# Memory attention, dense MoE and soft MoE in one kernel: five of eight chunks of M by VectorE turns, logits for two chunks at a time in the last batch, and another cut of the output stores

## The chip, the cores and the metric

The kernel runs on one core of a Trainium2 chip. The metric is device time in microseconds (us) of one execution. A core has a matrix engine (TensorE, PE in the profile, with its weight loads as PEld), VectorE (DVE), ScalarE (ACT), GpSimd (POOL) and SyncE (SP). DMA transfers are issued from a queue of an engine: here all of them are issued from SP's.

## The reference, cut to what matters

Three stages follow each other. `S` is 576 rows per batch, there are 4 batches.

```python
a = softmax(phi, axis=2)                       # over 32 memory slots
k_m, v_m = einsum(a, k), einsum(a, v)          # 32 x 64 per head
x = softmax(q @ k_m.T / 8) @ v_m               # attention, then heads side by side: (2304, 512)

p = domain_probs / domain_probs.sum(-1)
out = sum(p[:, e:e+1] * (relu(x @ w1[e]) @ w2[e]) for e in range(4))    # w1 512x1024, w2 1024x512

logits = out @ phi2                            # 32 slots
d = softmax(logits, axis=0); slot_input = d.T @ out
slot_out[e] = relu(slot_input[e] @ v1[e]) @ v2[e]                       # 8 experts, 4 slots each
return softmax(logits, axis=1) @ slot_out      # (2304, 512)
```

## The kernel before, in words

`out` of the middle stage is never built. The kernel keeps the hidden values h of the four experts and uses `M = w2 @ phi2` (32 columns for each of the 4096 hidden units, held as eight chunks of 512 units) so that the logits come straight from h. The slot input is gathered from h and multiplied by w2 only at the end.

The work on a batch goes in chunks n = 0 to 7, two for each expert. For each chunk, `g_mult` multiplies w1 by the batch's memory values (L695, with copies L704 and L706), and four `up` steps make h: each runs six matmuls of 288 columns for every half of the batch (L770 to L772), a ScalarE relu into an `hts` tile (L778), a VectorE 32x32 block turn into h (L784), and a GpSimd multiplication by the expert's share (L788). `logits` (L806; L813 in the last batch) multiplies the four `hts` tiles of a chunk by M and adds two chunks of an expert in one PSUM bank, which `expert` reads (L891). `group` then makes the column softmax of a batch and sums h with it (L976). Batches 0 to 2 are one unit each with both halves of the rows; the last batch is two units of 288 rows, and for these `logits` runs after each chunk, with four matmuls of 32x288.

`m_chunk` makes a chunk of M while batch 0 runs: one 1 MB load of w2 by SP, 16 TensorE transposes of 128x128 in four groups (L837) that ScalarE and VectorE copy out (L847, L843), four matmuls against phi2 (L854), a ScalarE copy (L860), four matmuls that fold and turn the result (L866) and a VectorE copy into M (L871). The chunks use the places R[3] and R[4] in turn, so a chunk's load waits until the chunk two before it has been read.

After the last `group` the end stage streams w2, v1 and v2 from memory in 1 MB blocks (`load_block`, `refill`) through buffers that the main loop gives up, makes the 32 slot outputs, and multiplies them by the row softmax: 20 result blocks of up to 128x512 (L1361, one PSUM bank each), copied out by VectorE (L1366) and ScalarE (L1369) in turn, and sent by SP (L368). The slot outputs lie in `so4`, whose left half ScalarE copies (L1347) and whose right half VectorE copies (L1349).

The order of the instructions on every engine is written by a planner (`Plan`): each step has an engine, an assumed cost, what it reads and writes, and a due time `at`; the planner plays the program through with these and puts each engine's steps out in the order in which they start there. On the chip every engine, SP's queue too, works through its list in that order and waits at a step whose input is late. Places in SBUF that a step may choose from (`uses`) are given out by `Uses` from the lifetimes in the order of due times.

## Time and profile before

| | us |
|---|---|
| median of 3 runs | 508.97 (508.2 to 511.94) |
| the profiled execution, device time | 507.71 |
| its span, first to last instruction | 505.9 |
| PE busy in the span | 476.3 |
| output stores in the span | 12, of 4.72 MB together |

The profiled execution is a fourth one. The profile gives the busy time of each engine, a chain of work followed back from the last instruction (each piece is what the next one waited for, or the instruction before it on its engine), the instructions grouped by line and shape, and the busy time, granted TensorE clock and DMA traffic of any stretch. The lines that the chain names tell the stages: L837 to L871 belong to M, L770 to L772 to `up`, L813 to the last batch's logits, L1361 to the result.

### The profile page before, as it was taken

To read this page: it belongs to the slowest core of one execution; us is meant where nothing else is said; L and a number is where in the kernel's file an instruction comes from. 1 tells how busy PE (TensorE), PEld (TensorE's weight loads), DVE (VectorE), ACT (ScalarE), POOL (GpSimd) and SP (SyncE) were. 2 spreads that over 40 slices of the span, in tenths; PEclk is the share of its full clock that TensorE was granted. 3 is DMA by queue.
4 is the path that set the end of the run, shared out by engine and by line. 5 is a ranking of instruction groups with operands and counts; after the bars stand their busy time and mean duration, and the time that the engine had idled before them with its cause. 6 is when DMAs were issued, how large, how long until landed. Compare 5 with 4: busy or idle time off the path is not lost.

```text
span 505.9 us, 13222 instructions
## 1 busy us (share of the span) xinstructions
PE 476.3 (94%) x5592; PEld 338.2 (67%) x5592; DVE 297.1 (59%) x605; ACT 202.7 (40%) x475; POOL 212.1 (42%) x255
## 2 busy tenths in 40 slices
PE   3999999999999999999999999999999989999971
PEld 2677787777876788788668887775687866333230
DVE  6588546656685857767684676586677553100032
ACT  2354445555550555455245555433543330010031
POOL 0244224546651348775324778532773850000000
PEclk9999999999999999999999999999999999899996
DMA  7999866415420946362082645525345988999938
GB/s 223 235 352 315 331 173 204 153 34 179 165 85 4 319 118 185 106 188 84 3 265 86 205 168 179 197 85 195 97 130 202 356 302 328 412 426 419 421 127 332
DMA packets 65243, 106.08 MB, mean 210 GB/s; under 512 B 28576, under 2 KB 40864, under 8 KB 59552
## 3 DMA queue, kind: packets, MB, share of 16 engines
q1 hardware_dynamic: 65184, 105.23, 60.9%
q8 instruction: 44, 0.72, 0.6%
q14 instruction: 15, 0.12, 0.1%
HBM read 100.50 MB, written 4.72 MB: 208 GB/s over the span
## 4 chain that ended last, share of the span: by engine, by line
PE 78%; DMA 14%; SPq 3%; DVE 2%; ACT 1%; issue 1%; DVEq 0%; ACTq 0%
PE ps L770 15%; PE ps L771 13%; PE ps L772 13%; PE ps L976 8%; DMA v<-in_moe_w_dram 8%; PE ps L695 6%; PE ps L806 5%; DMA h<-in_moe_w_dram 3%; PE ps L837 3%; SPq L368 3%; DMA raw<-in_moe_w_dram 3%; PE ps L813 2%; PE ps L854 2%; PE ps L603 2%; PE ps L615 2%; PE ps L866 1%
## 5 line engine op out<-in xcount | busy, mean ns | idle before, releaser
L788 POOL TENSOR_TENSOR h<-h,pe 128x576 f32<-128x576 f32 (+1 forms) x160 | 157.7, 996 | 141.5 <-DVE h L784 117.6
L770 PE MATMUL ps<-A,g 128*128 128x288 f32 x512 | 158.0, 309 | 0.2 <-ACT hts L778 0.2
L778 ACT ACTIVATE hts<-ps 128x288 f32<-128x288 f32 x256 | 105.1, 412 | 130.4 <-PE ps L772 129.0
L771 PE MATMUL ps<-A,g 128*128 128x288 f32 x512 | 151.1, 295 | 0.0
L772 PE MATMUL ps<-A,g 128*128 128x288 f32 x512 | 150.9, 295 | 0.0
L784 DVE STREAM_TRANSPOSE h<-hts 128x576 f32<-128x576 f32 (+1 forms) x160 | 102.4, 647 | 53.5 <-ACT hts L778 53.0
L770 PEld LDWEIGHTS ps<-A,g 128*128 128x128 f32 x512 | 96.1, 188 | 23.9 <-issue 18.6
L771 PEld LDWEIGHTS ps<-A,g 128*128 128x128 f32 x512 | 96.2, 188 | 0.3 <-POOL A L657 0.2
L772 PEld LDWEIGHTS ps<-A,g 128*128 128x128 f32 x512 | 96.1, 188 | 0.0
L706 DVE TENSOR_TENSOR g<-ps,g 128x512 fp32r<-128x512 f32 x64 | 41.0, 678 | 20.0 <-ACT g L704 19.9
L704 ACT CAST g<-ps 128x512 fp32r<-128x512 f32 x64 | 34.9, 590 | 34.5 <-PE ps L695 33.8
L976 PE MATMUL ps<-h,dts 32*32 32x512 f32 x1152 | 40.0, 597 | 1.6 <-DVE dts L958 1.6
L695 PE MATMUL ps<-raw,vbs 64*32 64x512 f32 x512 | 35.9, 600 | 1.6 <-DVE g L706 0.9
L976 PEld LDWEIGHTS ps<-h,dts 32*32 32x32 f32 x1152 | 22.8, 103 | 15.2 <-issue 4.6
L806 PE MATMUL ps<-hts,M 128*32 128x288 f32 x384 | 28.2, 411 | 0.0
L632 POOL TENSOR_TENSOR atts<-atts,small 128x256 f32<-128x256 f32 (+1 forms) x20 | 11.5, 575 | 25.7 <-DVE small L630 25.6
L837 PE MATMUL ps<-ident,h 128*128 128x128 f32 x128 | 18.1, 278 | 0.2 <-DVE g L706 0.2
L806 PEld LDWEIGHTS ps<-hts,M 128*32 128x32 f32 x384 | 10.4, 109 | 10.6 <-issue 5.1
L643 POOL TENSOR_TENSOR atts<-atts,small 128x256 f32<-128x256 f32 (+1 forms) x20 | 11.5, 575 | 13.4 <-DVE small L641 6.3
L837 PEld LDWEIGHTS ps<-ident,h 128*128 128x128 f32 x128 | 14.5, 143 | 2.4 <-issue 1.4
L894 POOL TENSOR_TENSOR lts<-lts,pe 128x288 f32<-128x288 f32 x15 | 10.4, 691 | 12.6 <-DMA v<-in_moe_w_dram 9.4
L657 POOL TENSOR_TENSOR A<-atts,A 128x256 fp32r<-128x256 f32 (+1 forms) x20 | 13.6, 680 | 4.4 <-ACT A L655 4.4
(185 smaller groups left out, 508.6 us busy)
## 6 DMA issues: line engine op xcount, KB each, us to landing
raw<-in_moe_w_dram SPq DMA_DIRECT2D x32, 1024.0 KB, 5.2
v<-in_moe_w_dram SPq DMA_DIRECT2D x20, 1024.0 KB, 12.5
h<-in_moe_w_dram SPq DMA_DIRECT2D x18, 1024.0 KB, 8.4
h<-in_k_dram SPq DMA_DIRECT2D x8, 512.0 KB, 5.2
h<-in_v_dram SPq DMA_DIRECT2D x8, 512.0 KB, 7.1
atts<-in_moe_w_dram SPq DMA_DIRECT2D x4, 1024.0 KB, 9.0
atts<-in_q_dram SPq DMA_DIRECT2D x12, 256.0 KB, 5.6
atts<-in_phi_dram SPq DMA_DIRECT2D x8, 256.0 KB, 4.7
```

The costliest lines, as they stand in the source:

```text
L695: nc.tensor.matmul(bank[bs[c]][32 * i:32 * i + 32, :], vb[b % 2][64 * c:64 * c + 64, 32 * i:32 * i + 32], t()[64 * c:64 * c + 64, i, :], s ...
L704: add(ACT, act(512), lambda c=c, src=src: nc.scalar.copy(out=placed(g()[:, 2 * c]), in_=src), r=[pk(bs[c])], w=[wk(o + 1024 * c, 512)], at ...
L706: add(DVE, dve(512), lambda c=c, src=src: nc.vector.tensor_tensor(out=placed(g()[:, 2 * c + 1]), in0=src, in1=placed(g()[:, 2 * c].bitcast ...
L770: nc.tensor.matmul(t, gh, ah, start=(c == 0), stop=False)
L771: nc.tensor.matmul(t, gh, al, start=False, stop=False)
L772: nc.tensor.matmul(t, gl, ah, start=False, stop=(c == 1))
L778: add(ACT, act(w), lambda: nc.scalar.activation(out=t[:, o0 - base:o1 - base], in_=bank[bm][:, 0:w], func=ACTF.Relu,), r=[pk(bm)], w=[wk(h ...
L784: add(DVE, dve(width), lambda: nc.vector.transpose(out=h_of(u, e)[:, kx], in_=t), r=[wk(ho, width)], w=[hk], at=at + 0.4)
L788: add(POOL, pool(width), lambda: nc.gpsimd.tensor_tensor(out=h_of(u, e)[:, kx], in0=h_of(u, e)[:, kx], in1=share, op=ALU.mult), r=["pe"], ...
L806: nc.tensor.matmul(lb[r0:r0 + 32, 0:HB], M[:, 4 * n + a, :], at_place(hos[a] + o0, o1 - o0), start=(first and h == 0), stop=(not first and ...
L837: nc.tensor.transpose(bank[bk][:, 128 * c:128 * c + 128], wn()[:, a, 128 * c:128 * c + 128], ident)
L976: nc.tensor.matmul(bank[S0 + p][32 * c:32 * c + 32, :], dtv[rows, tb, :], h_pair(u, ep)[rows, :, :, tb, :], start=(tb < 2), stop=(tb >= nt ...
```

## The change

It has three parts. Chunks 3 to 7 of M (the fourth to the eighth) no longer use `m_chunk` but a new `m_turned`: w2's chunk is loaded in four pieces of 32 partitions and 256 KB each, in runs of 1 KB; VectorE turns it in four block transposes of 128x512; TensorE makes 32 matmuls of 64 rows, 32 output partitions and 128 columns from a second copy of phi2 (`load_phi2`, four small loads), into one bank, the first 64 rows into its lower and the other 64 into its upper half; VectorE turns the result into M. For the last batch, `logits` runs after every second chunk, with the eight matmuls of both; `hts` places are then handed out in steps of 288. In the end stage the first row block of batches 0 and 1 is made in two column halves, the blocks are sent in other pieces and another order (`send`), and the four remainders of 64 rows are sent earlier in that order, from GpSimd's queue.

```diff
--- before.py
+++ after.py
...
@@ -364,8 +361,8 @@
     small_at.o = 0
-    def dma(to, of, size, r=(), w=(), at=0.0, cost=0.6):
-        add(SP, cost, lambda: nc.sync.dma_start(
+    def dma(to, of, size, r=(), w=(), at=0.0, cost=0.6, eng=SP):
+        add(eng, cost, lambda: (nc.sync if eng == SP else nc.gpsimd).dma_start(
             out=to() if callable(to) else to, in_=of() if callable(of) else of,
         ), r=r, w=w, at=at, size=size)
@@ -772,7 +769,8 @@
                 nc.tensor.matmul(t, gl, ah, start=False, stop=(c == 1))
         add(PE, 0.81, f, r=[wk(go, 2048)] + a_part(b, 0, o0, w) + a_part(b, 1, o0, w), w=[pk(bm)], at=at, lag=None)
         if ki == 0:
-            ht_of[u, n, fb] = uses(*[HT + 576 * n for n in range(NHT)])
+            step = 576 if len(ranges) == 2 else 288
+            ht_of[u, n, fb] = uses(*range(HT, HT + 576 * NHT, step), width=step)
         ho = ht_of[u, n, fb]
         t = at_place(ho, width)
         add(ACT, act(w), lambda: nc.scalar.activation(
@@ -794,7 +792,8 @@
         base = ranges[0][0]
         first = n % 2 == 0
         lb = bank[LB]
-        hos = [ht_of[u, n, a] for a in range(4)]
+        n0 = n if len(ranges) == 2 else n - 1
+        hos = [ht_of[u, m, a] for m in range(n0, n + 1) for a in range(4)]
         def f():
             if len(ranges) == 2:
@@ -809,15 +808,68 @@
                                 start=(first and h == 0), stop=(not first and h == 1),
                             )
             else:
-                for a in range(4):
+                for m, ho in enumerate(hos):
                     nc.tensor.matmul(
-                        lb[32 * a:32 * a + 32, 0:HB], M[:, 4 * n + a, :], at_place(hos[a], HB),
-                        start=first, stop=not first,
+                        lb[32 * (m % 4):32 * (m % 4) + 32, 0:HB], M[:, 4 * n0 + m, :], at_place(ho, HB),
+                        start=m < 4, stop=m >= 4,
                     )
         width = ranges[-1][1] - base
-        add(PE, 1.05 * len(ranges) / 2 + 0.05, f,
-            r=[("M", n)] + [wk(o, width) for o in hos], w=[pk(LB)], at=at, lag=0)
+        add(PE, 1.1, f,
+            r=[("M", m) for m in range(n0, n + 1)] + [wk(o, width) for o in hos], w=[pk(LB)], at=at, lag=0)
+    def phi_of():
+        return at_place(R[4] + 4096, 256).rearrange("p (c s) -> p c s", c=8)
+    def load_phi2(at):
+        for p in range(4):
+            dh = p % 2
+            dma(
+                lambda p=p: phi_of()[32 * p:32 * p + 32],
+                phi2[256 * dh:256 * dh + 256].rearrange("(c i) s -> i c s", i=32),
+                32768, w=[("phi2", p)] + ([wk(R[4] + 4096, 256)] if p == 0 else []), at=at,
+            )
+    def m_turned(n, ats):
+        e, f = divmod(n, F // FH)
+        o = R[3 + n % 2]
+        def wn(q, w):
+            return at_place(o + 512 * q, 512 * w)
+        def wt():
+            return at_place(o + 2048, 2048).rearrange("p (y a c h x) -> p h c a x y", y=2, a=4, c=8, h=2)
+        for p in range(4):
+            fh, dh = divmod(p, 2)
+            src = w2[e, FH * f:FH * f + FH, 256 * dh:256 * dh + 256]
+            src = src.rearrange("(h x k) d -> h x k d", h=2, k=8)[fh]
+            dma(
+                lambda p=p: wn(0, 4)[32 * p:32 * p + 32].rearrange("p (k d) -> p k d", k=8), src,
+                262144, w=[("wn", o, p)] + ([wk(o, 2048)] if p == 0 else []), at=ats[0] + 0.001 * p,
+            )
+        for a in range(4):
+            add(DVE, dve(512), lambda a=a: nc.vector.transpose(
+                out=at_place(o + 2048 + 512 * a, 512), in_=wn(a, 1)),
+                r=[wk(o + 512 * a, 512)] + [("wn", o, p) for p in range(4)],
+                w=[wk(o + 2048 + 512 * a, 512)], at=ats[1 + a])
+        bk = g_bank()
+        def part():
+            for c in range(8):
+                for q in range(4):
+                    rows = slice(64 * (q // 2), 64 * (q // 2) + 64)
+                    nc.tensor.matmul(
+                        bank[bk][32 * q:32 * q + 32, 0:128], phi_of()[rows, c, :], wt()[rows, q % 2, c],
+                        start=(c == 0), stop=(c == 7),
+                    )
+        add(PE, 2.3, part, r=[wk(o + 2048, 2048), wk(R[4] + 4096, 256)] + [("phi2", p) for p in range(4)],
+            w=[pk(bk)], at=ats[5])
+        add(DVE, 0.3, lambda: nc.vector.transpose(
+            out=M[:, 4 * n:4 * n + 4].rearrange("p a s -> p (a s)"), in_=bank[bk][:, 0:128],
+        ), r=[pk(bk)], w=[("M", n)], at=ats[5] + 0.1)
@@ -1148,9 +1201,10 @@
         add(PE, 0.3, lambda x=x, bk=bk: spread(x, bk), r=["dpn", "cst"], w=[pk(bk)], at=2.5 + x)
         add(DVE, 1.1 if x == 3 else 0.5, lambda x=x, bk=bk: tables(x, bk), r=[pk(bk)], w=["pe"], at=2.6 + x)
+    load_phi2(6)
     m_at = [2.5, 6.2, 10.5, 14.5, 18.5, 22.5, 26.5, 30.5]
     for n, m0 in enumerate(m_at):
-        m_chunk(n, [m_at[n - 2] + 1.6 if n > 1 else n - 181.5, m0, m0 + 0.5, m0 + 1, m0 + 1.5, m0 + 2.4, m0 + 3.2])
+        (m_chunk if n < 3 else m_turned)(n, [m_at[n - 2] + 1.6 if n > 1 else n - 181.5, m0, m0 + 0.5, m0 + 1, m0 + 1.5, m0 + 2.4, m0 + 3.2])
@@ -1172,7 +1226,8 @@
                     up(u, n, fb, ki)
             if u < NU - 1 and s + 1 < NG:
                 g_mult(s + 1, place(u, n, 1) + 0.1)
-            logits(u, n, place(u, n + 1) + (0.6 if n < NCH - 1 else 1.6))
+            if n % 2 or len(ranges) == 2:
+                logits(u, n, place(u, n + 1) + (0.6 if n < NCH - 1 else 1.6))
             if n % 2:
                 expert(u, n // 2, place(u, n + 1) + 1.7)
         z = starts[u + 1]
@@ -1354,46 +1409,57 @@
     spare = spare[:5]
     nres = [0]
-    def result(b, o, rows_out, ot, ok, at):
+    def result(b, o, rows_out, ot, cs, ok, at):
         rows = slice(32 * b, 32 * b + 32)
         bk = uses(*MM, LB, S0, S0 + 1, S0 + 2, S0 + 3)
-        m = rows_out.stop - rows_out.start
+        m, w = rows_out.stop - rows_out.start, cs.stop - cs.start
         add(PE, 0.3, lambda: nc.tensor.matmul(
-            bank[bk][0:m, :], ct[rows, o:o + m], so4[rows, :], start=True, stop=True,
-        ), r=[("ct", b), ("so4", 0), ("so4", 1)], w=[pk(bk)], at=at)
+            bank[bk][0:m, 0:w], ct[rows, o:o + m], so4[rows, cs], start=True, stop=True,
+        ), r=[("ct", b)] + [("so4", n) for n in range(2) if cs.start < 256 * n + 256 and 256 * n < cs.stop],
+            w=[pk(bk)], at=at)
         nres[0] += 1
         if nres[0] % 2:
-            add(DVE, dve(512), lambda: nc.vector.tensor_copy(out=ot(), in_=bank[bk][0:m, :]), r=[pk(bk)],
+            add(DVE, dve(w), lambda: nc.vector.tensor_copy(out=ot(), in_=bank[bk][0:m, 0:w]), r=[pk(bk)],
                 w=[ok], at=at + 0.01)
         else:
-            add(ACT, act(512), lambda: nc.scalar.copy(out=ot(), in_=bank[bk][0:m, :]), r=[pk(bk)], w=[ok],
+            add(ACT, act(w), lambda: nc.scalar.copy(out=ot(), in_=bank[bk][0:m, 0:w]), r=[pk(bk)], w=[ok],
                 at=at + 0.01)
+    def send(b, r0, r1, at):
+        t, o = spare[b]
+        dma(
+            out[b * S:b * S + 512, :].rearrange("(p r) d -> p r d", r=4)[:, r0:r1, :],
+            lambda: t()[:, r0:r1, :], 262144 * (r1 - r0), r=[wk(o + 512 * r0, 512 * (r1 - r0))], at=at,
+        )
     at = zz + 3
-    for r0 in (0, 2):
-        for b0 in (0, 2):
-            for x in range(2):
-                for b in (b0, b0 + 1):
-                    t, o = spare[b]
-                    i = r0 + x
-                    result(b, 128 * i, slice(0, 128), lambda t=t, i=i: t()[:, i, :], wk(o + 512 * i, 512), at)
+    whole_row = (slice(0, 512),)
+    for bs, rs in (((0, 1), (0,)), ((2, 3), (0, 1)), ((0, 1), (1,)), (None, None), ((0, 1), (2, 3)), ((2, 3), (2, 3))):
+        if bs is None:
+            t, o = spare[4]
+            for b in range(B):
+                rows_out = slice(64 * (b % 2), 64 * (b % 2) + 64)
+                k_ = ("tail", b)
+                result(
+                    b, 512, rows_out, lambda t=t, b=b, rows_out=rows_out: t()[rows_out, b // 2, :], whole_row[0], k_, at
+                )
+                dma(
+                    out[b * S + 512:b * S + 576, :], lambda t=t, b=b, rows_out=rows_out: t()[rows_out, b // 2, :],
+                    131072, r=[k_], w=[wk(o + 512 * b, 512)], at=at + 0.05, cost=1.0, eng=POOL,
+                )
+                at += 0.1
+            continue
+        for i in rs:
+            for b in bs:
+                t, o = spare[b]
+                for cs in halves if (b, i) in ((0, 0), (1, 0)) else whole_row:
+                    result(
+                        b, 128 * i, slice(0, 128), lambda t=t, i=i, cs=cs: t()[:, i, cs], cs,
+                        wk(o + 512 * i + cs.start, cs.stop - cs.start), at,
+                    )
                     at += 0.1
-            for b in (b0, b0 + 1):
-                t, o = spare[b]
-                dma(
-                    out[b * S:b * S + 512, :].rearrange("(p r) d -> p r d", r=4)[:, r0:r0 + 2, :],
-                    lambda t=t, r0=r0: t()[:, r0:r0 + 2, :], 524288, r=[wk(o + 512 * r0, 1024)], at=at,
-                )
-    t, o = spare[4]
-    for b in range(B):
-        rows_out = slice(64 * (b % 2), 64 * (b % 2) + 64)
-        k_ = ("tail", b)
-        result(b, 512, rows_out, lambda t=t, b=b, rows_out=rows_out: t()[rows_out, b // 2, :], k_, at)
-        dma(
-            out[b * S + 512:b * S + 576, :], lambda t=t, b=b, rows_out=rows_out: t()[rows_out, b // 2, :], 131072,
-            r=[k_], w=[wk(o + 512 * b, 512)], at=at + 0.05,
-        )
-        at += 0.1
+        for b in bs:
+            send(b, rs[0], rs[-1] + 1, at)
```

The order that comes out of the planner differs at these places. TensorE, batch 0, around a chunk of M. `ps_96` and `ps_97` are the two banks that M and g_mult share, `h_103` is the place of w2's chunk, L837 and L889 the transposes, L854 and L866 the product and the fold, L864 the new product. Before (the last group of transposes of one chunk, its product and its fold, with batch 1's memory sums L514 between them):

```order
L837 MATMUL ps_97<-ident,h_103 128x128 x4
L557 MATMUL ps_98<-ident,atts 128x128
L514 MATMUL ps_99<-h_89,atts 32x64 x16
L519 MATMUL ps_99<-atts 32x64 x4
L854 MATMUL ps_96<-h_103,phi_sb 32x512 x4
L514 MATMUL ps_98<-h_89,atts 32x64 x16
L519 MATMUL ps_98<-atts 32x64 x4
L866 MATMUL ps_97<-si,ct 128x32 x4
```

Now (two chunks' products follow each other, then the memory sums L511 and the next g_mult L692):

```order
L768 MATMUL ps_93<-A,g 128x288
L769 MATMUL ps_93<-A,g 128x288
L864 MATMUL ps_97<-h_103 32x128 x32
L864 MATMUL ps_96<-h_103 32x128 x32
L511 MATMUL ps_98<-h_89,atts 32x64 x16
L516 MATMUL ps_98<-atts 32x64 x4
L692 MATMUL ps_97<-raw,vbs 32x512
```

The product of a chunk is one row of 32 matmuls where a group of transposes, a product and a fold stood, and all eight chunks are through after 25 `up` steps of one half, where they took 38.

VectorE at about the same place of the program (L784 and L782 are the turns of h, L843 copies a group of transposes out, L871 and L924 copy M, L706 and L703 make g, L891 and L944 read the logits). Before:

```order
L784 STREAM_TRANSPOSE h_89<-hts 128x576
L871 COPY M<-ps_97 128x128
L891 STREAM_TRANSPOSE lts<-ps_95 128x288
L843 COPY h_103<-ps_97 128x4x128 x2
L561 COPY kbs<-ps_98 64x128 x2
L871 COPY M<-ps_97 128x128
L784 STREAM_TRANSPOSE h_89<-hts 128x576 x2
L706 TENSOR_TENSOR g<-ps_96,g 128x512
```

Now (L854 are the turns of w2, L870 those of the product into M):

```order
L924 COPY M<-ps_97 128x128
L854 STREAM_TRANSPOSE h_103<-h_103 128x512
L944 STREAM_TRANSPOSE lts<-ps_95 128x288
L854 STREAM_TRANSPOSE h_103<-h_103 128x512 x2
L870 STREAM_TRANSPOSE M<-ps_96 128x128
L854 STREAM_TRANSPOSE h_103<-h_103 128x512 x3
L782 STREAM_TRANSPOSE h_89<-hts 128x576
L854 STREAM_TRANSPOSE h_103<-h_103 128x512 x2
```

Six turns of w2 stand between two turns of h (the first of these is one row ahead of the piece), and a turn of w2 waits for its chunk's load. SP now issues the five chunks as 20 loads, the last two chunks ahead of batch 2's phi, where they stood behind it, and phi2's second copy as four more around batch 1's phi.

SP at the end of the program, the stores. Before:

```order
L368 DMA h_89<-in_moe_w_dram 128x2048 x2
L368 DMA out_dram<-h_89 128x1024 x2
L368 DMA out_dram<-atts 128x1024 x2
L368 DMA out_dram<-h_89 128x1024 x2
L368 DMA out_dram<-atts 128x1024 x2
L368 DMA out_dram<-v 64x512 x4
```

Now, with the four stores of 64x512 in GpSimd's list:

```order
L365 DMA out_dram<-h_89 128x512 x2
L365 DMA out_dram<-atts 128x1024 x2
L365 DMA out_dram<-h_89 128x512 x2
L365 DMA out_dram<-h_89 128x1024 x2
L365 DMA out_dram<-atts 128x1024 x2
```

The first two stores are half as large, and the remainders are no longer the last.

## Rows read from the trace of the kernel before

**Rows 1.** The page: TensorE's busy time, and the chain's shares by engine.

```profile
PE 476.3 (94%) x5592; PEld 338.2 (67%) x5592; DVE 297.1 (59%) x605; ACT 202.7 (40%) x475; POOL 212.1 (42%) x255
...
PE 78%; DMA 14%; SPq 3%; DVE 2%; ACT 1%; issue 1%; DVEq 0%; ACTq 0%
```

**Rows 2.** Stretches (us): length, busy per engine, granted clock, DMA share, GB/s.

```profile
60.00:90.00 30.00, 29.94 (x354) 24.06 (x351) 16.57 (x31) 14.61 (x32) 10.64 (x11) 1.00 0.66 204
432.00:488.00 56.00, 51.70 (x348) 17.51 (x340) 3.60 (x15) 4.46 (x8) 0.00 (x0) 0.97 0.93 384
420.00:425.00 5.00, 4.37 (x80) 2.88 (x62) 2.73 (x7) 0.00 (x0) 0.00 (x0) 1.00 0.55 184
```

**Rows 3.** The chain of waits from 61.5 to 111 us, shares by line.

```profile
by line: PE ps L837 18.9%; PE ps L770 14.1%; PE ps L771 12.3%; PE ps L772 12.3%; PE ps L854 10.3%; PE ps L866 10.0%; PE ps L806 6.4%; PE ps L695 5.2%; PE ps L603 4.1%; PE ps L615 3.1%; ACT ct L860 1.2%; PE ps L514 1.2%; PE ps L519 0.5%; PE 
```

**Rows 4.** The chain: four transposes of M, and the logits at 25 up steps.

```profile
61.90 0.47 PE ps L837 x4
...
81.17 0.97 PE ps L806 x16
```

**Rows 5.** The chain: 16 instructions of 128x32 by 128 columns.

```profile
76.16 0.59 PE ps L615 x16
...
88.80 0.47 PE ps L615 x16
```

**Rows 6.** Groups by line and shape: count, busy us, mean ns, idle before.

```profile
L784 DVE STREAM_TRANSPOSE h<-hts 128x576 f32<-128x576 f32 x96 | 73.6, 768 | 37.4 <-ACT hts L778 37.0
...
L784 DVE STREAM_TRANSPOSE h<-hts 128x288 f32<-128x288 f32 x64 | 28.8, 467 | 16.1 <-ACT hts L778 16.0
...
L843 DVE COPY h<-ps 128x512 f32<-128x512 f32 x16 | 10.9, 679 | 5.5 <-PE ps L837 5.3
```

**Rows 7.** Stretches as in rows 2: the loads of M, the stores.

```profile
46.00:60.00 14.00, 13.78 (x183) 10.02 (x181) 9.32 (x17) 6.65 (x15) 3.59 (x3) 1.00 0.99 348
492.00:502.00 10.00, 2.79 (x18) 0.67 (x14) 4.00 (x7) 3.22 (x7) 0.00 (x0) 0.77 1.02 406
502.00:505.00 3.00, 0.00 (x0) 0.00 (x0) 0.00 (x0) 0.00 (x0) 0.00 (x0) 0.50 0.70 219
```

**Rows 8.** Timeline: a chunk's transposes, and the issue of its load.

```profile
54.33 1.07 PE L837 MATMUL ps<-ident,h 128*128 128x128 f32 x8 [0.22 <-DVE g L706]
46.33 2.15 SPq L368 DMA_DIRECT2D h<-in_moe_w_dram  x2
```

**Rows 9.** Groups by shape: the last batch's logits.

```profile
L813 PE MATMUL ps<-hts,M 128*32 128x288 f32 x128 | 11.6, 418 | 0.0
```

**Rows 10.** The chain: logits of 16 instructions, and the next up's pieces.

```profile
324.06 1.11 PE ps L806 x16
325.17 0.33 PE ps L770
325.89 0.14 PE ps L771
```

**Rows 11.** The chain: logits of 8 instructions, and the next up.

```profile
391.94 0.62 PE ps L813 x8
392.57 0.33 PE ps L770
```

**Rows 12.** Timeline of the end: start, length, engine, line, what.

```profile
487.42 0.37 ACT L1347 COPY kbs<-ps 128x256 f32<-128x256 f32 x1 [0.79 <-PE ps L1343]
...
488.45 6.33 PE L1361 MATMUL ps<-kbs,ct 32*128 32x512 f32 x40 [0.61 <-DVE kbs L1349]
...
489.58 0.69 DVE L1366 COPY h<-ps 128x512 f32<-128x512 f32 x1 [1.27 <-PE ps L1361]
489.67 0.59 ACT L1369 COPY h<-ps 128x512 f32<-128x512 f32 x1 [1.87 <-PE ps L1361]
...
491.16 0.82 SPq L368 DMA_DIRECT2D out_dram<-h  x2
...
499.15 3.86 SPq L368 DMA_DIRECT2D out_dram<-v  x4
```

More of the change, by code (lines that the diff above doesn't have):

```diff
@@ L157, in __init__, with __call__ @@
         self.found, self.kinds = None, []
-    def __call__(self, *places):
+    def __call__(self, *places, width=1):
         uid = len(self.kinds)
-        self.kinds.append(places)
+        self.kinds.append((places, width))
         return Use(self.found[uid] if self.found else places[0], uid)
@@ L170, in settle @@
                     life.setdefault(uid, [n, n, s[0], s[0]])[1::2] = [n, s[0]]
-        taken = {}
-        found = {}
-        order = sorted(life, key=lambda uid: (len(self.kinds[uid]) > 1, life[uid]))
+        taken, found = [], {}
+        order = sorted(life, key=lambda uid: (len(self.kinds[uid][0]) > 1, life[uid]))
         for uid in order:
             a, z = life[uid][:2]
+            places, width = self.kinds[uid]
             best = None
-            for place in self.kinds[uid]:
-                held = taken.setdefault(place, [])
-                if all(z < lo or hi < a for lo, hi, _ in held):
-                    last = max((hi for _, hi, _ in held if hi < a), default=-1)
+            for place in places:
+                held = [h for h in taken if h[2] < place + width and place < h[2] + h[3]]
+                if all(z < h[0] or h[1] < a for h in held):
+                    last = max((h[1] for h in held if h[1] < a), default=-1)
                     if best is None or last < best[0]:
                         best = (last, place)
-            assert best is not None, (
-                self.kinds[uid], life[uid],
-                [(life[o][2:], o) for p in self.kinds[uid] for lo, hi, o in taken[p] if not (z < lo or hi < a)],
-            )
+            assert best is not None, (places, life[uid])
             found[uid] = best[1]
-            taken[best[1]].append((a, z, uid))
+            taken.append((a, z, best[1], width))
         self.found, self.kinds = found, []
@@ L839, in flip @@
                     )
-            add(PE, 0.42, flip, r=[wk(o + 512 * a, 512), "cst"], w=[pk(bk)], at=ats[1 + a])
+            add(PE, 0.42, flip, r=[wk(o + 512 * a, 512), "cst"] + [("wn", o, p) for p in range(4)], w=[pk(bk)],
+                at=ats[1 + a])
             src = bank[bk].rearrange("p (c f) -> p c f", c=4)
```

1 line of the change is left out of this document (removed).

## The prediction

> **What bounds the kernel now.** I read the page first: TensorE is busy for 476 of 505.9 us, and the chain that ends last is 78% TensorE and 14% DMA [rows 1]. A share of the whole span says nothing about one stage, so I took stretches next. From 60 to 90 us, where M is made beside batch 0, TensorE is busy 29.94 of 30 us while VectorE has 16.57 and the DMA engines a share of 0.66: only TensorE's work counts there, as long as data come in time. From 432 to 488 us it is the other way round: DMA share 0.93 at 384 GB/s [rows 2], the stream of w2, v1 and v2, where TensorE's time is worth nothing. Between the two, at 420 to 425 us, the DMA share is 0.55 [rows 2]: no transfers are left over when the last batch's sums end, so the stream starts as soon as these free its buffers, and what the main loop saves ahead of it moves the end one for one. Last I read the chain itself for M's steps, the logits and the stores.
>
> **M's chunks 3 to 7, what goes.** The chain from 61.5 to 111 us holds these five chunks and nothing of the first three. Of its 49.5 us, the transposes L837 take 18.9%, the product L854 10.3%, the fold L866 10.0%, and the wait for ScalarE's copy L860 1.2% [rows 3]: 9.4 + 5.1 + 5.0 + 0.6 = 20.0 us, or 4.0 a chunk. One group of a chunk's transposes stands in [rows 4].
>
> **What comes on TensorE.** A chunk has 32 matmuls, 64 instructions in the profile's two passes. The nearest rows are L615: 8 matmuls of 32 output partitions and 128 columns, 16 instructions, in 0.47 or 0.59 us [rows 5], four at a time in the four column groups. Four times that is 1.9 to 2.4 us; I take 2.1. It could not be had for less than 1.9, since the columns and the groups are the same. The other end is 3.8, twice 1.9, if the products from the lower 64 rows do not run beside those from the upper 64; no row shows two row halves writing one bank. Five chunks: 10.5 us, a gain of **9.5 us**.
>
> **What comes elsewhere.** A turn of 512 columns lies between VectorE's 467 ns for 288 and 768 for 576 [rows 6]: 0.70 us. 20 of them are 14.0 us; the 10 copies L843 that go, at 0.68 [rows 6], are 6.8. 7 us more on VectorE fit into its 13 idle us of the stretch, but its list is strict: a turn that waits for its load holds up the turn of h behind it, then the `hts` places, then `up`. ScalarE only loses copies. SP gets 19 more issues; two loads took it 2.15 us at 46 us [rows 8], so these may hold its queue for up to 20 us, spread over the 50 in which it now waits for other things, with w1's blocks and batch 1's k and v behind them. The M transposes at 54.33 us waited for VectorE's L706, not for their load [rows 8], so the loads are in time now, but from 46 to 60 us the DMA engines are full, share 0.99 at 348 GB/s [rows 7].
>
> **Late data.** The five chunks are wanted earlier (the order ends M after 25 `up` steps, today 81 us [rows 4], not 38), and in pieces of 32 partitions with 1 KB runs. No row has such a load. The nearest are the stores at the end: 128 partitions run at 406 GB/s for a share of 1.02, the 64-partition remainders at 219 for 0.70 [rows 7], 398 against 313 for a full share. So 1 MB costs 2.6 us of DMA at best and, as a bound, twice that. Twice it is 13 us more for five chunks, against 10 idle us of 60 to 90 (0.34 of 30): 3 us that nothing covers, and some waits out of turn. Between 0 and 3 I take **+1.5 us**. On this the Trainium skill, page "SBUF — State Buffer", section "Door 1: The DMA port swizzle", speaks against the change: 32 partitions reach 8 of 16 ports, and it lists 189 GB/s for 1 MB there against 328 for 128 partitions. By it five loads would take 1.7 times as long, 9.5 us more and nearly all of the idle time; I would then put the term at 2 and the sum below at -11.5, where the 128-partition rate alone gives 0 and -13.5.
>
> **The last batch's logits.** 128 instructions are 16 steps of 8 [rows 9], each 0.62 us, and the first piece of the next `up` is 0.33 instead of the usual 0.14 [rows 10, 11]. Merged, 16 instructions take 1.11 [rows 10]: 16 x 0.62 - 8 x 1.11 = 1.0 us, and 0.2 for each switch that goes. Of 8, I count 6, since g_mult breaks the `up` steps at some of these places anyway: 1.2. Together **-2.2 us**, between -1.0 and -2.7. Cover is not needed: it is all TensorE's own time. The steps of the eight tiles hold `hts` longer, but there are now 12 places of 288 columns; if VectorE fell behind, `up` would wait for a place.
>
> **The stores.** Now the first result matmul starts at 488.45, the first copy at 489.58, and the first store goes out at 491.16, after two rounds of copies of 0.69 us [rows 12]. With halves, the left one needs only ScalarE's copy, done at 487.79 (487.42 + 0.37), and the right one starts as today; of the lag of 1.13 us about half goes with the columns. So the right half is copied from 489.0 to 489.6 on, 0.35 us long, and the first store goes at about 489.7, 1.5 us sooner. The DMA engines then drain 4.72 MB at 406 GB/s without a gap until 502, and carry the remainders at 219 to 505 [rows 7]. The two first stores are 0.52 MB, 1.3 us of that; a gap of a few tenths may follow, since the next four blocks need two more rounds. The remainders, now in the middle, may give back up to 1.4 of their 3 us. Between -1.0 and -2.7 I take **-1.8 us**. GpSimd's store is an operation that this trace does not have. SP's remainders go out from 499.15 on [rows 12]; the new ones can go some 6 us sooner, so a GpSimd issue that is 6 us slower than SP's costs nothing, and a faster one gains nothing, as the stream is full.
>
> **Sum:** -9.5 + 1.5 - 2.2 - 1.8 = -12.0 us on a profiled execution of 507.71, so 495.7. The median of the runs is 1.26 us above that execution, so I forecast **497.0 us** against 508.97.
>
> **Rivals.**
> - *A, data in time and everything at its good end:* gains of 10.5, 2.7 and 2.7 us, 493 us. For it: DMA has idle time and VectorE too. Chance 0.08 for below 493.
> - *B, M's gain goes into waits for its data:* VectorE's strict list stands behind each load, so that a late chunk costs `up` as well as its own product. 1.3 us at each of five products beyond the 1.5 makes 6.5: 503.5. For it: the DMA engines are full at 46 to 60 us, and the order wants M a third sooner. Against it: 10 idle us behind. Chance 0.14.
> - *C, the two row halves take turns:* 3.8 instead of 2.1 us for five products is 8.5 us, less the late data that this covers: 504. For it: all other row-split matmuls of this kernel write a bank for each row group. The Trainium skill, page "TensorEngine Tiling (Array Packing)", section "Gotcha 1: PSUM Pressure", has it as a rule that row tiles cannot access one bank at the same time; by it C would hold, or the halves would have to be kept apart in another way. Against it: the halves write different partitions. Chance 0.10.
> - *D, slower than before:* pieces of 32 partitions move at a quarter of the rate of 128, about 100 GB/s. 1 MB then takes 10 us; the five, which share two places, come in one row from 48.5 us on [rows 8], with two blocks of w1 of 2.6 us between them. The last lands at 104 and is turned at 107, where TensorE, at 25 `up` steps, stands at about 83, 2 us later than today [rows 4] for the products that are moved ahead. It waits 24 us in one sum: 497 - 1.5 + 24 is 519.5. It decides from about 8 us a chunk on; the 64-partition stores, at 0.8 of the rate for a full share, are far from that. Chance 0.04.
> - That the change does not do what it says is out: the order has five products, eight merged logits, and the new stores.
>
> The forecast itself, from 493 to 501, has 0.64. The range takes in most of B and the middle of C, **492.5 to 504**: outside lie some of A, the upper ends of B and C, and D, together about 0.2. 1% is 5.1 us, which is about what a measurement tells from no change. Below 503.9 lie the forecast, A, half of B and half of C: faster 0.85; the rest of B and C within 1%: 0.11; slower 0.04.
>
> **What would show it.** In the changed profile: a product of M (L864) of 32 matmuls at 1.9 to 2.4 us (C: near 3.8); no line between 28 and 90 us in which TensorE waits for VectorE or a load for more than 1.5 us in all (B and D: waits of L864 for the turns L854, and of these for w2); eight merged logits of 1.1 us; the first store 1.5 us after the first result matmul or less, and the DMA engines full from there to the end; GpSimd's stores landing before SP's last. The forecast is wrong if M's loads come late by more than their chunk's product, if the stream of v1 and v2 does not start as much sooner as TensorE finishes, or if GpSimd's stores end last.

## The result and the profile after

The changed kernel is **slower**, by 0.9%: 513.62 us median (511.63 to 513.86) against 509.36 for the kernel before on the same chip, a ratio of 1.0086 (95% interval 1.0072 to 1.0100). Forecast were 497.0 us with a range of 492.5 to 504. The profiled execution took 513.68 us, its span 511.9. In this section and the next, 1% is 5.1 us.

The page, TensorE's busy time and the chain's shares by engine; it answers to [rows 1]:

```profile
PE 471.8 (92%) x5756; PEld 339.0 (66%) x5756; DVE 303.5 (59%) x616; ACT 193.4 (38%) x461; POOL 214.4 (42%) x259
...
PE 69%; DMA 20%; DVE 4%; SPq 3%; issue 1%; ACT 1%; DVEq 0%; ACTq 0%
```

TensorE works less than before, but the chain has 20% DMA where it had 14%, and TensorE's share fell from 78% to 69%. The place is found with one row per stage: the sums that open the column softmax of batch 0 (the first matmul of `group`), in the kernel before and in the changed one:

```profile
145.59 0.76 PE L918 MATMUL ps<-lts,rr 64*128 64x288 f32 x4
```

```profile
154.36 0.76 PE L971 MATMUL ps<-lts,rr 64*128 64x288 f32 x4
```

Batch 0, where M is made, ends 8.8 us later. From there to the last batch's final sums (L927 before at 413.24, L980 now at 419.19) it is 264.8 us instead of 267.7, so the logits gave 2.8. One pair of executions tells the first of these numbers only roughly: the traces of the kernels below that share logits and stores agree from there on within 0.8 us, but batch 0 ends at 145.6 us in the kernel before and at 146.8 to 150.2 in the three that change only its stores. From the fold of the slot outputs (486.68 before, 492.67 now) to the end it is 19.2 us in both: the stores gave nothing.

Stretches of the changed kernel, columns as in [rows 2]; the first two answer to its first two rows, the third to the first of [rows 7]:

```profile
60.00:90.00 30.00, 25.70 (x462) 20.60 (x462) 17.74 (x35) 5.91 (x13) 5.44 (x5) 0.91 0.95 212
432.00:488.00 56.00, 53.78 (x375) 19.46 (x374) 6.12 (x20) 4.73 (x8) 0.00 (x0) 0.97 1.01 421
46.00:60.00 14.00, 10.37 (x94) 7.27 (x92) 8.79 (x14) 5.75 (x13) 3.93 (x4) 0.95 1.13 308
```

From 60 to 90 us TensorE now has 4.3 idle us, and the DMA engines are full (0.95) at hardly more GB/s than they moved before at 0.66. From 28 to 112 us as a whole TensorE is busy for 71.6 of 84 us, before for 83.6.

The chain of waits in that stretch (start, length, what). It covers the stretch of [rows 3], where it was TensorE's own work but for a wait of 1.2% for ScalarE:

```profile
26.74 9.76 DMA atts<-in_phi_dram
...
48.73 11.94 DMA h<-in_moe_w_dram
60.67 0.14 issue
60.80 1.94 PE ps L889 x8
...
71.62 7.88 DMA h<-in_moe_w_dram
79.63 1.30 DVE h L854 x2
80.94 0.66 DVE h L782
81.59 1.20 DVE h L854 x2
...
85.22 10.05 DMA h<-in_moe_w_dram
95.40 2.49 DVE h L854 x4
97.94 0.83 issue
98.77 0.77 DVE h L782
99.54 0.59 DVE g L703
100.17 4.52 PE ps L864 x128
```

Four waits for loads stand in it: batch 1's phi, the third chunk of w2 (still one load of 128 partitions), and two sets of pieces. Behind the pieces the turns of w2 (L854) stand in VectorE's list, and behind these the turn of h (L782) and g (L703), which `up` and the next product wait for. The waits say the same; a row is engine, line, what it waited for: us in all, times, longest:

```profile
DVE h L854 <- DMA h<-in_moe_w_dram: 13.4, 4, 5.8
...
PE ps L889 <- DMA h<-in_moe_w_dram: 4.4, 1, 4.4
...
PE ps L864 <- DVE g L703: 3.2, 2, 2.8
```

The last row of the chain is two products of M: 2.26 us each. A pair of chunks' merged logits in the chain, and the first piece of the next `up`, for [rows 11]:

```profile
394.86 1.11 PE ps L812 x16
395.97 0.33 PE ps L767
```

16 instructions take 1.11 us, as in [rows 10], where two steps of 0.62 stood.

The end in stretches, for [rows 7] and [rows 12]; the first is the three us from the issue of the first store on:

```profile
495.51:498.51 3.00, 3.00 (x22) 1.07 (x19) 2.76 (x5) 2.59 (x6) 0.00 (x0) 1.00 0.66 250
498.00:501.00 3.00, 2.42 (x16) 0.91 (x12) 2.95 (x6) 2.66 (x6) 2.26 (x4) 1.00 1.01 394
501.00:504.00 3.00, 0.00 (x0) 0.00 (x0) 0.51 (x1) 0.29 (x1) 0.00 (x0) 0.72 1.04 277
504.00:510.00 6.00, 0.00 (x0) 0.00 (x0) 0.00 (x0) 0.00 (x0) 0.00 (x0) 0.50 0.94 360
```

The first store goes out at 495.51, 2.84 us after the fold instead of 4.48, but the engines then have a gap. In the same three us of the kernel before they were fuller, 0.74 instead of 0.66:

```profile
491.16:494.16 3.00, 3.00 (x18) 1.18 (x20) 3.00 (x6) 2.73 (x6) 0.00 (x0) 1.00 0.74 294
```

While the remainders move, the rate is 277 GB/s at a full share.

### The profile page after: what moved, and what is told of

The parts are those of the page before. It is cut to its first block, busy times and chain, and to the rows that moved or that the text cites. A ratio compares the mean times of both kernels' runs of the same rounds, so it can differ in the third digit from the quotient of the medians.

```text
span 511.9 us, 13568 instructions
## 1 busy us (share of the span) xinstructions
PE 471.8 (92%) x5756; PEld 339.0 (66%) x5756; DVE 303.5 (59%) x616; ACT 193.4 (38%) x461; POOL 214.4 (42%) x259
## 4 chain that ended last, share of the span: by engine, by line
PE 69%; DMA 20%; DVE 4%; SPq 3%; issue 1%; ACT 1%; DVEq 0%; ACTq 0%
PE ps L767 13%; PE ps L769 12%; PE ps L768 12%; DMA h<-in_moe_w_dram 9%; PE ps L1029 8%; DMA v<-in_moe_w_dram 8%; PE ps L692 5%; PE ps L805 5%; SPq L365 3%; DMA atts<-in_phi_dram 2%; PE ps L600 2%; PE ps L612 2%; PE ps L812 2%; DMA h<-in_q_dram 2%; PE ps L889 1%; PE ps L1416 1%
## 5 line engine op out<-in xcount | busy, mean ns | idle before, releaser
L786 POOL TENSOR_TENSOR h<-h,pe 128x576 f32<-128x576 f32 (+1 forms) x160 | 157.9, 995 | 146.8 <-DVE h L782 114.5
L782 DVE STREAM_TRANSPOSE h<-hts 128x576 f32<-128x576 f32 (+1 forms) x160 | 102.5, 647 | 44.5 <-ACT hts L776 44.1
L703 DVE TENSOR_TENSOR g<-ps,g 128x512 fp32r<-128x512 f32 x64 | 41.0, 678 | 17.1 <-ACT g L701 17.1
L692 PE MATMUL ps<-raw,vbs 64*32 64x512 f32 x512 | 36.1, 611 | 0.6 <-DMA raw<-in_moe_w_dram 0.6
L365 POOL DMA_DIRECT2D out_dram<-v x4 | 2.3, 570 | 80.3 <-ACT v L1425 80.3
L854 DVE STREAM_TRANSPOSE h<-h 128x512 f32<-128x512 f32 x20 | 12.8, 679 | 13.4 <-DMA h<-in_moe_w_dram 13.4
L947 POOL TENSOR_TENSOR lts<-lts,pe 128x288 f32<-128x288 f32 x15 | 10.3, 687 | 15.5 <-DMA v<-in_moe_w_dram 9.6
```

Source lines behind the costliest of these rows:

```text
L365: add(eng, cost, lambda: (nc.sync if eng == SP else nc.gpsimd).dma_start(out=to() if callable(to) else to, in_=of() if callable(of) else o ...
L692: nc.tensor.matmul(bank[bs[c]][32 * i:32 * i + 32, :], vb[b % 2][64 * c:64 * c + 64, 32 * i:32 * i + 32], t()[64 * c:64 * c + 64, i, :], s ...
L703: add(DVE, dve(512), lambda c=c, src=src: nc.vector.tensor_tensor(out=placed(g()[:, 2 * c + 1]), in0=src, in1=placed(g()[:, 2 * c].bitcast ...
L782: add(DVE, dve(width), lambda: nc.vector.transpose(out=h_of(u, e)[:, kx], in_=t), r=[wk(ho, width)], w=[hk], at=at + 0.4)
L786: add(POOL, pool(width), lambda: nc.gpsimd.tensor_tensor(out=h_of(u, e)[:, kx], in0=h_of(u, e)[:, kx], in1=share, op=ALU.mult), r=["pe"], ...
```

## The experiments

Ratios are to the kernel before, with their 95% intervals. Of each edit the lines that matter are shown, with `...` for the others. The first four part the change and try the first cause.

**Logits alone.** The kernel before with the new `logits` and places only.

```diff
-            logits(u, n, ...)
+            if n % 2 or len(ranges) == 2:
+                logits(u, n, ...)
```

> The kernel before with one part of the change alone: the last batch's logits for two chunks per step (and places of 288 columns). Theory 1, the forecast's term is right and M alone turned the sum over: 2.2 us faster, ratio 0.9955. Rival, the stages move as a whole and the merged logits only shift the wait: ratio 1.000. In the changed kernel the time from the end of batch 0 to the last batch's final sums is 2.8 us shorter than before, which speaks for theory 1.

0.9929 (0.9914 to 0.9944), 505.94 us: 3.6 us faster. The merging pays, by somewhat more than either theory. Its trace has 264.8 us from batch 0's column softmax to the last batch's final sums, as the changed kernel; the traces with the old logits have 267.6 to 267.7. So 2.8 us are the logits' own, and the rest lies in batch 0, where executions of one kernel differ.

**Stores alone.** The kernel before with the new `result`, `send` and remainders from GpSimd.

```diff
+    for bs, rs in (((0, 1), (0,)), ((2, 3), (0, 1)), ((0, 1), (1,)), (None, None), ...
+                    131072, ..., eng=POOL,
```

> The kernel before with the new result blocks and stores alone. The forecast's term: 1.8 us faster, ratio 0.9965. Theory from the changed kernel's trace, where the first store starts 1.5 us sooner but the DMA engines then run below their full rate and end 18.1 us after the first result matmul where they took 17.4: ratio 1.000 to 1.002, no gain.

1.0005 (0.9988 to 1.0022): no gain, as the second theory has it. Its profiled execution is the slowest of twelve (512.24 us, median 508.92); batch 0 ends at 150.19 us in it with M made as before.

**Both, with M in the old way.**

```diff
-        (m_chunk if n < 3 else m_turned)(n, ...)
+        m_chunk(n, ...)
```

> The changed kernel with all chunks of M in the old way. Theory, M's new loads are the whole loss and the two other parts only add: 2.2 to 2.8 us faster than before from the logits and 0 to 0.6 us lost at the stores, ratio 0.995 to 0.997, and so some 6.5 us faster than the changed kernel. Rival, the loss is spread over the parts: ratio above 1.000.

0.9939 (0.9922 to 0.9957), 506.40 us. The two parts add. So M's part alone costs 1.0086 / 0.9939, 1.5% or 7.5 us, where the forecast had it gain 8.0 (9.5 less the 1.5 of late data).

**The chunk in one load.**

```diff
-        for p in range(4):
-            ...
+        dma(wn(0, 4)..., w2[e, FH * f:FH * f + FH].rearrange("(p k) d -> p k d", k=4), 1048576, ...)
```

> The changed kernel, but each turned chunk of w2 comes in one load over 128 partitions in runs of 8 KB, the same 1 MB (the rows of w2 then lie in other partitions, so M of these chunks is not the reference's). Theory S, the shape of the pieces halves the rate of the DMA engines and this alone makes the data late: most of the forecast comes, ratio 0.975 to 0.985. Rival O, the chunks are wanted too early for SP's queue and for the two places, whatever the shape: within 2 us of the changed kernel, ratio 1.005 to 1.009.

0.9883 (0.9864 to 0.9903), 504.04 us. 10 of the 15.5 us between the forecast gain and the loss come back. This lies between the ranges of the two theories: the shape of the pieces is most of what went wrong and not all of it, and M's part now gains 2.9 us, not 8. Two stretches of this kernel show some of what is left:

```profile
36.00:40.00 4.00, 2.09 (x15) 1.61 (x14) 3.35 (x8) 0.66 (x2) 0.00 (x0) 1.00 0.42 60
40.00:44.00 4.00, 4.00 (x21) 2.21 (x19) 3.84 (x8) 1.06 (x3) 2.02 (x2) 0.57 0.97 356
```

TensorE idles for 1.9 us; the chain has a wait of 9.87 us for batch 1's phi up to 36.6 us there, as in the changed kernel, and the four us behind it run at a granted clock of 0.57.

**Partitions or run length.** Two kernels keep the four issues of 256 KB. One keeps the 32 partitions and makes the runs long; the other keeps the 1 KB runs and spreads each piece over 128 partitions.

```diff
+                ... w2[e, FH * f + 128 * p:FH * f + 128 * p + 128].rearrange("(x k) d -> x k d", k=4)
```

> The changed kernel, but each of the four pieces of a turned chunk brings its 32 partitions one run of 8 KB instead of eight of 1 KB: same bytes, same number of issues, same partitions (the rows of w2 lie elsewhere, so M of these chunks is not the reference's). Theory P, 32 partitions are what halves the rate: near the changed kernel, ratio 1.004 to 1.009. Theory R, the short runs are: near the whole load's 0.9883, ratio 0.988 to 0.993.

1.0051 (1.0031 to 1.0071).

```diff
+                ... wn(0, 4).rearrange("p (k g d) -> p k g d", k=4, g=2)[:, 2 * (p // 2):2 * (p // 2) + 2, p % 2]
```

> The changed kernel, but each of the four pieces goes to all 128 partitions in two runs of 1 KB each: same bytes, same number of issues, same run length (M of these chunks is not the reference's). Theory P, the 32 partitions halve the rate: near the whole load's 0.9883, ratio 0.988 to 0.993. Theory R, the short runs do: ratio 1.004 to 1.009. If neither recovers, the four issues by SP are what costs.

0.9898 (0.9874 to 0.9923), as good as the one load. From 70 to 73 us little but pieces moves in each of the three kernels. In turn the changed kernel, 32 partitions with long runs, and 128 partitions with short runs:

```profile
70.00:73.00 3.00, 3.00 (x66) 2.20 (x68) 0.96 (x2) 0.18 (x1) 1.19 (x1) 1.00 1.16 201
```

```profile
70.00:73.00 3.00, 3.00 (x77) 2.21 (x72) 0.52 (x2) 0.00 (x0) 1.19 (x1) 1.00 1.09 208
```

```profile
70.00:73.00 3.00, 3.00 (x31) 2.83 (x34) 2.56 (x6) 1.24 (x3) 0.00 (x0) 1.00 0.98 330
```

At a full share, 201 and 208 GB/s for 32 partitions, 330 for 128. Of the two, the number of partitions sets the rate; the run length is worth 1.8 us of the kernel's time, the partitions 9.6. The four issues cost nothing that shows.

**The planner told.** The pieces' size, which the planner divides by 0.33 MB/us, is entered 1.6 times as large.

```diff
-                262144, w=[("wn", o, p)] + ...
+                425000, w=[("wn", o, p)] + ...
```

> The changed kernel, but the planner is told that a piece takes 1.6 times as long (425000 bytes for 262144; what is loaded is the same), so that turns and products stand later in the lists. Theory, the wait is one of order, VectorE's turns standing ahead of data that cannot be there: 3 to 6 us come back, ratio 0.997 to 1.003. Rival, the DMA engines are full and any order ends batch 0 late: within 2 us of the changed kernel, ratio 1.005 to 1.012.

1.0001 (0.9982 to 1.0019): 4.3 us come back with the same loads, by other lists. VectorE's waits for w2 fall from 13.4 to 5.8 us:

```profile
DVE h L854 <- DMA h<-in_moe_w_dram: 5.8, 2, 3.3
```

**phi2's second copy.** Left out, and then only moved.

```diff
-    load_phi2(6)
```

> The changed kernel without the second copy of phi2 and its four loads; the products of the turned chunks read the first copy (so their M is not the reference's). Theory, the copy's short runs and issues make batch 1's phi and SP's queue late at 25 to 38 us, 1.3 idle us of TensorE and a low clock behind it: 1.5 to 3 us faster than the changed kernel, ratio 1.003 to 1.006. Rival, the copy is too small to matter: ratio 1.008.

1.0043 (1.0021 to 1.0065): 2.2 us back.

```diff
-    load_phi2(6)
+    load_phi2(12)
```

> The changed kernel with the second copy of phi2 due later (12 instead of 6), so that its four loads go out behind batch 1's k and v and no longer ahead of batch 1's phi. Theory, the copy's place in SP's queue is what cost the 2.2 us that its absence gave back: ratio 1.003 to 1.006. Rival, the gain came from the planner's other order on VectorE and TensorE: ratio 1.007 to 1.010.

1.0031 (1.0012 to 1.0050): 2.8 us back, so it is the copy's place, or the order that the planner makes with it there, and not its bytes. The traces say which. Batch 1's phi does not go out sooner with the copy late: SP begins its four loads at 27.55 us in this run and at 26.74 in the changed kernel. What differs is the order: with the copy early, the planner puts batch 1's k behind phi in SP's list (35.52 instead of 25.45 us) and the first step on phi (L454) ahead of the copies of M's transposes (L896) in VectorE's. The changed kernel, then this run:

```profile
36.52 1.04 DVE L454 TENSOR_REDUCE atts<-atts 128x128 f32<-128x512 f32 x1 [2.03 <-DMA atts<-in_phi_dram]
37.47 0.69 DVE L896 COPY h<-ps 128x512 f32<-128x512 f32 x1
```

```profile
34.91 0.69 DVE L896 COPY h<-ps 128x512 f32<-128x512 f32 x1 [0.69 <-PE ps L889]
39.65 2.04 DVE L454 TENSOR_REDUCE atts<-atts 128x128 f32<-128x512 f32 x2
```

The kernel before and the run without the copy have the second order. So the step on phi that stands ahead of M's copies, and waits there, goes with the loss; the copy does not hold phi back.

**Both halves of the partitions at once.** Two pieces from GpSimd's queue, or the pieces in another order.

```diff
+                ... eng=POOL if p > 1 else SP
```

> The changed kernel, but of each chunk's four pieces the two for partitions 64 to 127 are issued from GpSimd's queue and the two for 0 to 63 from SP's, so that pieces of both halves can move at the same time. Theory P as a matter of which partitions are written at a time: the pair moves nearer to the rate of 128 partitions, ratio 0.990 to 1.000. Rival, GpSimd's queue is no help (it issues late behind its own list, or its transfers are slow): ratio 1.005 or more.

1.0081 (1.0064 to 1.0098).

```diff
-        for p in range(4):
+        for p in (0, 2, 1, 3):
```

> The changed kernel with the four pieces of a chunk in another order on SP's queue, so that the halves of the partitions alternate (0 to 31, 64 to 95, 32 to 63, 96 to 127). If neighbouring pieces overlap in the queue they then write different halves: ratio 1.000 to 1.005. Rival, a piece moves by itself whatever follows: ratio 1.007 to 1.010.

1.0086 (1.0057 to 1.0116). Neither helps. In the first, both queues moved data from 68 to 72 us, 0.43 MB from GpSimd's and 0.52 from SP's, at 232 GB/s together:

```profile
68.00:72.00 4.00, 4.00 (x43) 2.75 (x42) 2.25 (x7) 1.00 (x2) 1.50 (x4) 1.00 0.98 232
```

From 72 to 76 us (packets, MB, share of 16 engines) it was mostly GpSimd's (q0):

```profile
q0 software_dynamic: 194, 0.61, 80.3%
q1 hardware_dynamic: 365, 0.16, 26.3%
```

So with pieces of both queues in flight the rate rose little over 201 to 208 GB/s and stayed far from 330. How much of the two halves was written at the same moment the trace does not tell.

**The corrections together.** The one load with the late copy:

```diff
+        dma(wn(0, 4)..., 1048576, ...)
...
+    load_phi2(12)
```

> The changed kernel with one load of 128 partitions for a turned chunk (M of these chunks is not the reference's) and the second copy of phi2 behind batch 1's k and v. With the whole load alone the ratio was 0.9883, some 3 us of M's forecast gain of 8. Theory, the rest went to phi2's copy, which holds batch 1's phi back: the two add, ratio 0.981 to 0.985. Rival, something else takes it (chunk 3's load beside chunk 2's, VectorE's list): 0.987 to 0.990.

0.9831 (0.9806 to 0.9856), 500.92 us. They add. M's part, against 0.9939 without it, now gains 5.5 us. The rows from 36 to 44 us, after those of the one load above:

```profile
36.00:40.00 4.00, 4.00 (x31) 2.69 (x29) 3.15 (x12) 1.41 (x3) 0.38 (x1) 1.00 0.86 207
40.00:44.00 4.00, 4.00 (x37) 4.00 (x35) 3.53 (x6) 1.99 (x4) 2.70 (x3) 1.00 1.01 363
```

TensorE's wait behind phi is gone, and the clock is full. The pieces as they are, with the planner told, the late copy and the old stores:

```diff
+                425000, w=[("wn", o, p)] + ...
...
+    load_phi2(12)
```

> The changed kernel with the old stores, with the planner told of the pieces' real time and phi2's copy behind k and v. If the three corrections add, from 1.0086: 1.0086 - 0.0085 - 0.0055 = 0.9946, less 0 to 0.001 for the stores, so 0.993 to 0.996, no better than the merged logits alone (0.9929), since the DMA engines stay full. Rival, they take from the same wait and add only in part: 0.997 to 1.000.

0.9903 (0.9876 to 0.9930), 504.94 us: better than either theory (the first one's range begins where the interval ends), and faster than both kernels, with the slow loads kept. Against the merged logits alone (0.9929) the intervals overlap, so a gain from M's part itself is not shown here.

**Fewer chunks** turned, the rest as in the run before, except that phi2's copy is due at 16 with three chunks and at 20 with two (12 with four). The edit with 5 turns three chunks, with 6 two, with 4 four.

```diff
-        (m_chunk if n < 3 else m_turned)(n, ...)
+        (m_chunk if n < 5 else m_turned)(n, ...)
```

> As the run before, but only the last three chunks are turned (6 to 8), and phi2's copy is due still later (16). Theory, the DMA engines have room for three chunks in pieces behind 65 us: the 1.7 to 1.9 us of TensorE saved by each come in full, 0.9929 - 3 x 0.0036 = 0.982 to 0.986. Rival, each chunk's late data takes its gain: 0.990 to 0.996.

0.9898 (0.9864 to 0.9933), 504.28 us: just under the rival's range, and far from the theory's.

> As the run before with only the last two chunks turned (phi2's copy due at 20). Theory, two chunks come in time: 0.9929 - 2 x 0.0036 = 0.985 to 0.988. Rival, no gain: 0.991 to 0.995.

0.9934 (0.9904 to 0.9963): the rival, no gain.

> The kernel with what the runs so far speak for: merged logits, the old stores, M's last four chunks turned (5 to 8), the planner told of the pieces' real time, phi2's copy due at 12. With five such chunks the ratio was 0.9903, where chunk 4's pieces moved beside chunk 3's load and TensorE waited 3.5 us for that load; with three it was 0.9898. Theory, with four the load of chunk 4 is whole and this wait goes: 0.985 to 0.989. Rival, the gain stays at that of the two neighbours: 0.989 to 0.992.

0.9979 (0.9961 to 0.9998): a miss for both theories. The waits are from the slowest of its twelve executions (510.28 us, median 507.85). The one for the whole chunk's load did not go (2.6 us), and there is one that the run with five chunks does not have, behind VectorE's list:

```profile
PE ps L864 <- DVE g L703: 4.5, 2, 3.6
PE ps L889 <- DMA h<-in_moe_w_dram: 2.6, 1, 2.6
```

A turn that waits for its pieces stands ahead of the subtraction that makes g, and the next product waits for that. With three chunks the gain over the logits alone (0.9929) lies inside the intervals, and with two there is none. That fewer chunks pay more is not shown. That the order of the lists alone can cost 4.3 us is, by the run with the planner told.

**The stores.** Alone again, with the remainders sent by SP at the same place, and then as the last.

```diff
-                    131072, ..., cost=1.0, eng=POOL,
+                    131072, ...,
```

> The kernel before with the new result blocks and stores, the four remainders issued from SP's queue at the same place instead of GpSimd's. With GpSimd's the ratio was 1.0005. Theory Q, the transfers from GpSimd's queue beside SP's are what costs the 1.5 us of the earlier start: 0.997 to 0.999. Rival, the gap behind the two small first stores and the 64 partitions cost it, whatever the queue: 0.9995 to 1.002.

0.9985 (0.9976 to 0.9995), in the range of theory Q.

```diff
-    ... ((0, 1), (1,)), (None, None), ((0, 1), (2, 3)), ((2, 3), (2, 3))):
+    ... ((0, 1), (1,)), ((0, 1), (2, 3)), ((2, 3), (2, 3)), (None, None)):
```

> The run before with the remainders as the last stores, as in the kernel before, behind the earlier start. Theory, the earlier start is worth its 1.5 us less the gap of 0.6: 0.9975 to 0.999. Rival, the end is set by what follows and no earlier start counts: 0.9995 to 1.001.

0.9984 (0.9970 to 0.9999). From the fold to the end it is 18.6 and 18.5 us, against 19.2 in the kernel before and in the run with GpSimd's remainders (18.9 to 19.7 in all the traces with them). SP's remainders are worth 0.6 us, their place nothing that shows. In the first, the three us from the issue of the first store on, and the remainders between the others:

```profile
490.81:493.81 3.00, 3.00 (x22) 1.07 (x18) 2.76 (x5) 2.59 (x6) 0.00 (x0) 1.00 0.51 193
497.00:500.00 3.00, 0.00 (x0) 0.00 (x0) 0.00 (x0) 0.00 (x0) 0.00 (x0) 1.00 0.97 294
```

At 0.51 where the kernel before has 0.74, the gap takes 0.7 us of the start, and the remainders move at 294 GB/s between the others.

## Why the prediction was wrong

**What goes and comes on TensorE was right.** A product takes 2.26 us (forecast 2.1, from [rows 5]), so five cost 11.3 us instead of the chain's 20.0. Rival C, which had 3.8, is out: the two row halves write one bank side by side. The page "TensorEngine Tiling (Array Packing)" of the Trainium skill, section "Gotcha 1: PSUM Pressure", has it that row tiles cannot share a bank at a time; here halves that write different partitions do.

**The step that failed is the late data, +1.5 us.** With TensorE's gain of 8.7 and a measured loss of 7.5, it was about +16: the idle DMA time of the old schedule was taken as cover, and in the new order it was none. Three things went wrong in it.

- *"13 us more for five chunks, against 10 idle us of 60 to 90 ... 3 us that nothing covers."* The size was about right: at the 201 GB/s measured a chunk takes 5.2 us, twice the 2.6 of the bound. Against loads on 128 partitions at 330 that is 2.0 us more a chunk, 10 in all. The cover was not. The 10 idle us were those of the old schedule, in which M took until 111 us. The new order asks for the same loads within a shorter time, in which the engines are full, and a chunk's load may go only when the chunk two before it has been read. The trace of before had this: the share was 0.99 at 46 to 60 us ([rows 7]), and the sum should have been made against the time in which the new order wants the data, not against an average of the old one. On 128 partitions the same data give 9.6 us back.
- *"the loads are in time now", "19 more issues ... spread over the 50".* I counted the issues but not what they do to the order. phi2's copy, where it stood, cost 2.2 to 2.8 us, with batch 1's k sent later and VectorE's step on phi ahead of M's copies; and the third chunk's load, which I left out since it does not change, took 11.94 us beside the pieces of the fourth. TensorE waited for it for 4.4 us.
- *The planner.* It counts 0.33 MB/us for every load, so it put turns and products where pieces at 0.2 could not be. I had read its rule and did not ask what a wrong cost would do. Telling it gave 4.3 us; with the copy moved as well and the old stores, 9.3. This overlaps with the first cause: a slow load costs much where the order does not expect it (the last of these kernels keeps the slow loads and is faster than before).

Rival B named the mechanism ("VectorE's strict list stands behind each load") and priced it at 6.5 us beyond the 1.5, less than half of what came. Rival D's mechanism, pieces so slow that TensorE waits, is what happened, from a lower price than its own: I had it decide from 8 us a chunk, and at 201 GB/s a chunk takes 5.2. It got 0.04. On the page "SBUF — State Buffer", section "Door 1: The DMA port swizzle", the Trainium skill lists 189 GB/s for 1 MB in 32 partitions against 328 for 128: the trace agrees, with 201 and 330. I cited this and changed the term by half a us, because the same cover stood against it.

**What the end depends on was right too:** batch 0 lost 8.8 us, the logits gave 2.8, and the end came 6.0 us later, one for one.

**The logits were right in kind:** -2.2 forecast, -2.8 between the stages of both traces, -3.6 (2.8 to 4.4) measured alone.

**The stores failed by two sizes.** The start came 1.6 us sooner, as forecast. "A gap of a few tenths" was 0.2 us here (a share of 0.66 instead of 0.74 over three us) and 0.7 in a run with SP's remainders, and the remainders in the middle gave nothing back (277 to 294 GB/s beside the others). That GpSimd's queue "costs nothing" was wrong by 0.6 us. This lies in the transfers: by the packets of the traces the last one ends 17.7 and 18.0 us behind the fold with GpSimd's remainders (changed kernel, stores alone), 17.2 and 17.0 with SP's, and 1.2 to 1.7 us of the span follow in every trace. Of the 1.6 us, some 0.8 is in neither the gap nor the queue and stays open.

What stays open: with loads at full rate and the late copy, M's part still gains 5.5 us where 8.7 of TensorE's work goes. TensorE's wait for the third chunk's load is 1.7 us in that kernel's profile (0.6 in that of both parts with M in the old way); the rest stays open.

## What to carry to other kernels

Price a new load shape by its rate, and then make the sum over the time in which the new order wants the data; idle DMA time of the old schedule covers nothing if the loads may not be issued in it. Where a planner writes the lists, give it the new shape's cost in the same change: here that, one load's place and the old stores turned 4.3 us of loss into 4.6 of gain, most of which (3.6) the merged logits give alone. A small load costs by what it does to the order of the lists, not by its bytes: look at what its place moves on the other engines too.

## What was not expected of the hardware

- The number of partitions, not the run length, set a load's rate: 201 to 208 GB/s for 32 partitions with runs of 1 and of 8 KB, 330 for 128 with runs of 1 KB, each at a full share.
- Waits cost twice, through the clock. In the changed kernel:

```profile
56.00:60.00 4.00, 0.37 (x3) 0.14 (x2) 1.27 (x2) 0.48 (x2) 1.18 (x1) 0.82 1.11 226
60.00:64.00 4.00, 3.20 (x48) 2.61 (x48) 0.69 (x1) 0.59 (x1) 0.00 (x0) 0.50 1.08 253
```

  TensorE stood still for 3.6 of 4 us, and its granted clock in the next four was 0.50, the lower level of 1.2 GHz. Eight instructions of L889 took 1.94 us there and 0.87 at 45.37 us of the same execution, where the granted clock was 1.00 (44 to 48 us).
